# Column mean of the weights from block sums on GpSimd, and the low words' top bits on ScalarE, in an attention and feed-forward kernel

## The chip, the cores and the metric

The kernel runs on one core of a Trainium2 chip. The metric is the device time of one execution in microseconds (us); the kernel before has a median of 963.42 us over 3 runs. The engines are named as in the profile: PE is TensorE (PEld its weight loads), DVE is VectorE, ACT is ScalarE, POOL is GpSimd, SP is the engine that issues most of the DMAs.

## The reference

```python
def reference(**kw):
    # q, k, v: (8 batches, 8 heads, 576 positions, 64), float32
    scores = q @ k^T / 8, masked: heads 0-3 the last 32 positions, heads 4-7 every 32nd position
    x = softmax(scores) @ v           # laid out as (8, 576, 512)
    return _moe_ref(x, g_ln, w_ch1, w_ch2)

def _moe_ref(x, g_ln, w_ch1, w_ch2):  # w_ch1 (512, 2048), w_ch2 (2048, 512): float64 as drawn
    mu = np.mean(x, axis=-1, keepdims=True)
    var = np.mean((x - mu) ** 2, axis=-1, keepdims=True)
    xn = (x - mu) / np.sqrt(var + 1e-06) * g_ln
    ch = np.maximum(xn @ w_ch1, 0.0) @ w_ch2
    return (x + ch).astype(np.float32)
```

The two weights reach the kernel as 64-bit floats, that is as pairs of 32-bit words: a low word and a high word.

## The kernel before, in words

The 8 x 576 rows of x are worked in 9 chunks of 512 rows (c = 0 to 8). The hidden dimension 2048 is worked in 16 blocks of 128 (f = 0 to 15). For each chunk and block, `ffn1` multiplies x by a block of the first weights into one PSUM tile `ph`, ScalarE takes the positive part into `hh` (line 651), VectorE the rest into `hl` (line 652), and one step later `ffn2` multiplies these by the block of the second weights. Weights and x are held as sums of two parts that TensorE multiplies fast, so that each product is three products.

The attention of the later batches is cut into pieces (a generator `pieces`). In every step f one piece stands between `ffn1(f)` and `ffn2(f-1)`: scores, a transposition of the probabilities, the product with v, or a transposition of the result. A piece has work on TensorE and, behind it, on VectorE, ScalarE and GpSimd. Some pieces also turn the next pair's q and k on VectorE (lines 362 to 367).

The weights are taken apart once, in chunk 0, by the class `Split`. A block has two halves: half 0 is its part of the first weights, half 1 of the second. For a half,

- `scaled` (ScalarE, line 188) scales the high word by a power of two into a PSUM tile `p`, of which there is a single buffer;
- `low` (VectorE, line 194) shifts the low word right by 29, in place;
- `magnitude` (VectorE, line 198) puts the two together, and `sign` (VectorE, line 204) adds the sign and writes the 32-bit weight `r`.

For half 0, `by_g` (GpSimd, line 212) multiplies the rows by the layer norm's factors into `wg`. `column_mean` (TensorE, line 219) multiplies `r` by `gmean`, a matrix that holds the factors over 512, so that each column's mean stands in all 128 rows of the PSUM tile `cm`; that takes four products, one for each block of 128 rows, and each of them is two passes in the trace. `centred` (VectorE, line 223) subtracts it from `wg`. `two_parts` writes a half's high part by ScalarE (line 234) and the rest by GpSimd (line 235).

In chunk 0, step f splits block g = f + 2 (`new`) and finishes block f + 1 (`old`), which `ffn1(f+1)` needs next. Blocks 0 and 1 are split by `whole()` ahead of step 0. Each engine keeps the order in which the code is written: the last lines of the kernel tie every instruction to the one before it on its engine. So the order of the calls in the step is the order on each engine. The PSUM tile `cm` and the pieces' PSUM tiles are in chunk 0 turns of one single buffer (`ps_a`): the mean of block g waits until the piece's tile has been read, and the next piece until `centred` has read `cm`.

Of the kernel before, what the change touches and what calls it, by code (L numbers as in the profile page):

```python
# [8 lines left out]
F32 = mybir.dt.float32  # L9
F32R = mybir.dt.float32r  # L10
U32 = mybir.dt.uint32
AF = mybir.ActivationFunctionType
ALU = mybir.AluOpType
AX = mybir.AxisListType
# [5 lines left out]
def kernel(  # L20
# [10 lines left out]
    nc = tc.nc  # L31

    B, H, S, D = q.shape
    DM, DFF = w1.shape
# [38 lines left out]
    mhalf = const.tile([P, 1], F32, name="mhalf")  # L73
    nc.gpsimd.memset(mhalf, -0.5)
    gcol = const.tile([P, NCC], F32, name="gcol")
    gmean = const.tile([P, NCC, P], F32, name="gmean")


    mask_l = const.tile([P, 64], F32, name="mask_l")
# [100 lines left out]
    class Split:  # L180
        def __init__(self, f):
            self.f = f
            self.bits = [t.rearrange("p (f t) -> p f t", t=2) for t in staged.pop(f)]
            self.p, self.w = [None, None], [None, None]

        def scaled(self, i):
# [3 lines left out]
                scale=2.0 ** -112)  # L190

        def low(self, i):
            t = self.bits[i][:, :, 0]
            nc.vector.tensor_scalar(t, t, 29, None, op0=ALU.logical_shift_right)

        def magnitude(self, i):
            t = self.p[i].bitcast(U32)
# [10 lines left out]
        def by_g(self):  # L208
            w = self.w[0].rearrange("p (c f) -> p c f", c=NCC)
            self.wg = tkp.tile([P, DM], F32, tag="tk", name=f"wg{self.f}")  # L210
            self.wgv = self.wg.rearrange("p (c f) -> p c f", c=NCC)
            nc.gpsimd.tensor_tensor(
                out=self.wgv, in0=w, in1=gcol.unsqueeze(2).broadcast_to([P, NCC, P]), op=ALU.mult)

        def column_mean(self):
            w = self.w[0].rearrange("p (c f) -> p c f", c=NCC)
            self.mean = bank(f"cm{self.f}")[:, 0:P]
            for c in range(NCC):
                nc.tensor.matmul(  # L219
                    self.mean, gmean[:, c, :], w[:, c, :], start=(c == 0), stop=(c == NCC - 1))  # L220

        def centred(self):
            nc.vector.tensor_tensor(
                out=self.wgv, in0=self.wgv,
                in1=self.mean.unsqueeze(1).broadcast_to([P, NCC, P]), op=ALU.subtract)

        def two_parts(self, i):
            w = (self.wg, self.w[1])[i]
            t = w_tile(i + 1, self.f, [P, 2, DM], F32R, "w")
            (w1s, w2s)[i][self.f] = t  # L230
            if i == 1 and self.f == NFC - 1:

                w_pools[1].tile([P, 88], F32, name="pad")
            nc.scalar.activation(out=t[:, 0], in_=w, func=AF.Copy)  # L234
            nc.gpsimd.tensor_tensor(out=t[:, 1], in0=w, in1=t[:, 0].bitcast(F32), op=ALU.subtract)  # L235

        def whole(self):
            self.low(0)
# [457 lines left out]
    for i in range(NHP + 3):  # L696
        if i < NHP:
            first[i].s_scores()
        if 2 <= i <= NHP + 1:
            first[i - 2].v_piece()  # L700
            if i < NHP:
                pairs[NHP + i - 2].load_v()
        if i + 1 < NHP:
            first[i + 1].t_rows()
        if 3 <= i:
            first[i - 3].x_piece()
        if 1 <= i <= NHP:
            first[i - 1].p_piece()
            first[i - 1].v_shifted()
        if i < NHP:  # L710
            first[i].s_exp()
        if i == NHP - 1:
            nc.vector.tensor_scalar(
                gmean, gcol.unsqueeze(2).broadcast_to([P, NCC, P]), 1.0 / DM, None, op0=ALU.mult)
        if i == NHP:
            Split(0).whole()
    w_late()
# [66 lines left out]
    for c in range(NCHUNK):  # L784
# [7 lines left out]
        for f in range(NFC):  # L792
            if c == 0:
# [5 lines left out]
                if new:  # L799
                    new.scaled(0)  # L800
                    new.low(0)
                if old:
                    old.centred()
                    old.two_parts(0)
                    old.two_parts(1)
                if new:
                    new.magnitude(0)
                    new.sign(0)
                    new.by_g()
                    new.low(1)  # L810
                    new.scaled(1)
            h = ffn1(c, f)
# [70 lines left out]
```

## Time and profile before

| | |
|---|---|
| median of 3 runs | 963.42 us (960.73 to 964.25) |
| the profiled execution | 962.39 us |
| its span, first to last instruction | 960.6 us |
| mean granted TensorE clock | 0.99 |
| busy: PE, DVE, ACT, POOL | 96%, 44%, 22%, 13% of the span |

The shares are means over the span. Chunk 0's steps run from about 55 to 175 us; behind them the weights are ready, and only the products and the rest of the attention are left. Rows of a timeline give start, length, engine, line, operation, output and inputs; a bracket at the end gives the engine's idle time before the instruction and what ended it. Two instructions that follow each other on an engine overlap a little, so that the step from start to start is shorter than the length.

### The profile page before, as it was taken

Reading aid. Unit: us, or ns where it says so; the run is one execution under the profiler, and the core shown is the slowest. Engines: PE = TensorE matmul, PEld = TensorE weight load, DVE = VectorE, ACT = ScalarE, POOL = GpSimd, SP = SyncE. Lnnn points to the kernel's source line nnn. Section 1 sums busy time; section 2 is a strip of 40 time slices with the busy share of each in tenths; the row PEclk is TensorE's granted clock in tenths of the full one; section 3 lists DMA queues with packets and bytes.
Section 4 is the critical chain, followed back from the end, with each engine's and each line's share of the span. In section 5 each row is a group of like instructions: output and inputs, shape, how many; then the busy total and the mean of one; then the engine's idle time right before and its main releaser. Section 6 shows DMA issues by size and latency. Waiting matters only on the chain.

```text
span 960.6 us, 18743 instructions
## 1 busy us (share of the span) xinstructions
PE 926.0 (96%) x7936; PEld 766.6 (80%) x7936; DVE 427.0 (44%) x857; ACT 212.6 (22%) x337; POOL 127.3 (13%) x150
## 2 busy tenths in 40 slices
PE   6669999999999999999999999999999999999997
PEld 6558787788888888888888888888888888888886
DVE  2689988633454334434543454335432331132112
ACT  3534444121111121211121211121111111110100
POOL 4245556100000001000100010001000000000000
PEclk9879999999999999999999999999999999999999
DMA  9866873442333334333433344334221121002001
GB/s 200 238 158 155 208 212 78 85 101 46 86 63 94 62 85 73 95 61 85 73 95 62 83 74 96 62 64 94 71 38 48 36 76 45 0 1 88 1 1 44
DMA packets 239427, 80.16 MB, mean 83 GB/s; under 512 B 190064, under 2 KB 232688, under 8 KB 239344
## 3 DMA queue, kind: packets, MB, share of 16 engines
q1 hardware_dynamic: 236128, 77.27, 35.3%
q10 hardware_dynamic: 3216, 1.71, 0.8%
q8 instruction: 62, 1.02, 0.5%
q14 instruction: 21, 0.17, 0.1%
HBM read 59.48 MB, written 19.46 MB: 82 GB/s over the span
## 4 chain that ended last, share of the span: by engine, by line
PE 89%; DMA 3%; DVE 3%; SPq 3%; issue 1%; ACT 1%; ACTq 0%; DVEq 0%
PE po L662 40%; PE ph L643 26%; PE ph L647 13%; PE m L464 2%; PE m L396 2%; SPq L299 2%; PE cm L219 2%; PE n L449 1%; PE n L536 1%; DMA rows<-in_k_dram 1%; DMA s<-in_moe_w_ch_dram 1%; DVE p L198 1%; SPq L170 1%; PE av L464 0%; DMA raw<-in_k_dram 0%
## 5 line engine op out<-in xcount | busy, mean ns | idle before, releaser
L662 PE MATMUL po<-w,hh 128*128 128x512 f32 x1152 | 362.2, 396 | 0.0
L652 DVE SCALAR_TENSOR_TENSOR hl<-ph,hh 128x512 fp32r<-128x512 f32 x144 | 99.6, 692 | 465.7 <-ACT hh L651 465.3
L662 PEld LDWEIGHTS po<-w,hh 128*128 128x128 f32 x1152 | 211.2, 188 | 43.6
L643 PE MATMUL ph<-xh,w 128*128 128x512 f32 x576 | 227.2, 395 | 0.2 <-ACT xh L559 0.2
L643 PE MATMUL ph<-xl,w 128*128 128x512 f32 x576 | 225.7, 392 | 0.2 <-DVE xl L561 0.2
L662 PE MATMUL po<-w,hl 128*128 128x512 f32 x576 | 224.9, 391 | 0.0
L651 ACT ACTIVATE hh<-ph 128x512 fp32r<-128x512 f32 x144 | 85.9, 597 | 488.8 <-PE ph L647 488.8
L647 PE MATMUL ph<-xh,w 128*128 128x512 f32 x576 | 154.4, 390 | 0.0
L643 PEld LDWEIGHTS ph<-xl,w 128*128 128x128 f32 x576 | 109.0, 189 | 22.8 <-DVE xl L561 0.5
L643 PEld LDWEIGHTS ph<-xh,w 128*128 128x128 f32 x576 | 108.9, 189 | 22.8 <-ACT xh L559 0.7
L647 PEld LDWEIGHTS ph<-xh,w 128*128 128x128 f32 x576 | 108.5, 188 | 22.7
L662 PEld LDWEIGHTS po<-w,hl 128*128 128x128 f32 x576 | 108.1, 188 | 23.3
L437 POOL TENSOR_TENSOR sm<-sm,mx 128x648 f32<-128x648 f32 (+1 forms) x32 | 40.6, 1269 | 420.2 <-DVE mx L432 409.9
L624 POOL TENSOR_TENSOR rs<-rs,mhalf 128x1 f32<-128x1 f32 x36 | 20.0, 554 | 342.3 <-DVE rs L623 342.3
L440 ACT ACTIVATE sm<-sm 128x648 f32<-128x648 f32 (+1 forms) x32 | 23.8, 744 | 138.7 <-POOL sm L437 138.6
L219 PE MATMUL cm<-r,gmean 128*128 128x128 f32 x128 | 19.3, 299 | 16.2 <-DVE r L204 11.3
L219 PEld LDWEIGHTS cm<-r,gmean 128*128 128x128 f32 x128 | 17.7, 208 | 19.1 <-issue 15.6
L561 DVE TENSOR_TENSOR xl<-n,xh 128x480 fp32r<-128x480 f32 (+2 forms) x36 | 22.7, 666 | 15.4 <-ACT xh L559 15.4
L188 ACT ACTIVATE p<-s 128x512 f32<-128x512 f32 x32 | 20.5, 642 | 34.5 <-DVE r L204 33.1
L432 DVE TENSOR_REDUCE mx<-sm 128x12 f32<-128x648 f32 (+1 forms) x32 | 26.4, 824 | 2.3
L513 DVE TENSOR_TENSOR xo<-m,den 64x64 f32<-64x64 f32 (+3 forms) x120 | 27.1, 290 | 0.1
L235 POOL TENSOR_TENSOR w<-wg,w 128x512 fp32r<-128x512 f32 x16 | 20.7, 1292 | 41.9 <-ACT w L234 38.8
(95 smaller groups left out, 645.9 us busy)
## 6 DMA issues: line engine op xcount, KB each, us to landing
s<-in_moe_w_ch_dram SPq DMA_DIRECT2D x32, 512.0 KB
out_dram<-x SPq DMA_DIRECT2D x32, 256.0 KB
raw<-in_q_dram SPq DMA_DIRECT2D x112, 72.0 KB
raw<-in_k_dram SPq DMA_DIRECT2D x112, 72.0 KB
xds<-xo SPq DMA_DIRECT2D x32, 162.0 KB
v_l<-in_v_dram SPq DMA_DIRECT2D x32, 144.0 KB
xdl<-xo SPq DMA_DIRECT2D x16, 256.0 KB
x<-xdl SPq DMA_DIRECT2D x32, 128.0 KB
```

Source lines behind the costliest of these rows:

```text
L219: nc.tensor.matmul(self.mean, gmean[:, c, :], w[:, c, :], start=(c == 0), stop=(c == NCC - 1))
L235: nc.gpsimd.tensor_tensor(out=t[:, 1], in0=w, in1=t[:, 0].bitcast(F32), op=ALU.subtract)
L432: nc.vector.reduce_max(mx[:, :, 0:nt], sm, axis=AX.X)
L437: nc.gpsimd.tensor_tensor(out=sm, in0=sm, in1=mx[:, :, 0:nt].unsqueeze(3).broadcast_to([P, 2, nt, w]), op=ALU.subtract)
L440: nc.scalar.activation(out=sm, in_=sm, func=AF.Exp, scale=SCALE)
L513: nc.vector.tensor_tensor(out=xo[r, t0:t1, h0:h1].rearrange("p t h d -> p h t d"), in0=av, in1=den[r, h0:h1, t0:t1].unsqueeze(3).broadcast_to(
L561: nc.vector.tensor_tensor(out=dst(xl), in0=src, in1=dst(xh).bitcast(F32), op=ALU.subtract)
L643: nc.tensor.matmul(ph, w1h[:, cc], x[:, cc, :], start=(n == 0), stop=False)
L647: nc.tensor.matmul(ph, w1l[:, cc], xh[:, cc, :], start=False, stop=(cc == NCC - 1))
L651: nc.scalar.activation(out=hh, in_=ph, func=AF.Relu)
L652: nc.vector.scalar_tensor_tensor(out=hl, in0=ph, scalar=0.0, in1=hh.bitcast(F32), op0=ALU.max, op1=ALU.subtract)
L662: nc.tensor.matmul(po[i], hx[:, cs], w, start=(f == 0 and n == 0), stop=(f == NFC - 1 and n == 2))
```

## The change

Three things are changed, all in `Split`.

- The column mean comes from block sums. Behind `by_g` GpSimd adds the four blocks of 128 columns of `wg` in two steps into `bsum` (128x256, then 128x128), and TensorE multiplies the sum once by a constant matrix of 1/512. The matrix `gmean` and the VectorE instruction that filled it are gone.
- `low` runs on ScalarE: it reads the top byte of the low word (one byte in eight), scales and shifts it, and writes the rounded integer to where VectorE wrote the shifted word.
- In a step, half 1 of the old block is finished first, and GpSimd's rest of half 0 comes behind the new block's `by_g` and sums. ScalarE's `low(1)` stands ahead of `scaled(1)`.

```diff
-    gmean = const.tile([P, NCC, P], F32, name="gmean")
+    mean = const.tile([P, P], F32, name="mean")
+    nc.gpsimd.memset(mean, 1.0 / DM)
+    bsum = const.tile([P, 2, P], F32, name="bsum")
+    const.tile([P, P], F32, name="gap")
...
+            self.top = [t.bitcast(U8).rearrange("p (f t) -> p f t", t=8)[:, :, 3] for t in st]
...
         def low(self, i):
-            t = self.bits[i][:, :, 0]
-            nc.vector.tensor_scalar(t, t, 29, None, op0=ALU.logical_shift_right)
+            nc.scalar.activation(
+                out=self.bits[i][:, :, 0], in_=self.top[i], func=AF.Copy, scale=1.0 / 32,
+                bias=-31.0 / 64)
...
                 out=self.wgv, in0=w, in1=gcol.unsqueeze(2).broadcast_to([P, NCC, P]), op=ALU.mult)
+            nc.gpsimd.tensor_tensor(
+                out=bsum, in0=self.wgv[:, 0:2], in1=self.wgv[:, 2:4], op=ALU.add)
+            nc.gpsimd.tensor_tensor(out=bsum[:, 0], in0=bsum[:, 0], in1=bsum[:, 1], op=ALU.add)

         def column_mean(self):
-            w = self.w[0].rearrange("p (c f) -> p c f", c=NCC)
             self.mean = bank(f"cm{self.f}")[:, 0:P]
-            for c in range(NCC):
-                nc.tensor.matmul(
-                    self.mean, gmean[:, c, :], w[:, c, :], start=(c == 0), stop=(c == NCC - 1))
+            nc.tensor.matmul(self.mean, mean, bsum[:, 0], start=True, stop=True)
...
-        if i == NHP - 1:
-            nc.vector.tensor_scalar(
-                gmean, gcol.unsqueeze(2).broadcast_to([P, NCC, P]), 1.0 / DM, None, op0=ALU.mult)
...
                 if old:
+                    old.two_parts(1)
                     old.centred()
-                    old.two_parts(0)
-                    old.two_parts(1)
+                    old.high(0)
                 if new:
                     new.magnitude(0)
                     new.sign(0)
                     new.by_g()
+                if old:
+                    old.rest(0)
+                if new:
                     new.low(1)
                     new.scaled(1)
```

`high(i)` and `rest(i)` are the ScalarE and the GpSimd half of `two_parts(i)`. The instructions of the chunks behind chunk 0, and those of the SP queue, stand as before.

On ScalarE this is step f = 4 before, which splits block 6 and finishes block 5 (`p_6` is the scaled word, `w_5` an old half's high part, from `wg` for half 0 and from `r` for half 1, `hh_4` the output of `ffn1(4)`, `pt_0` the piece's copy):

```order
L188 ACTIVATE p_6_1221<-s_6_924 128x512
L234 ACTIVATE w_5_1225<-wg_1128 128x512
L234 ACTIVATE w_5_1228<-r_5_1198 128x512
L188 ACTIVATE p_6_1237<-s_6_925 128x512
L651 ACTIVATE hh_4_1252<-ph_4_1239 128x512
L454 COPY pt_0_1263<-pp_0_1257 128x640
```

And the same step of the changed kernel (line 199 is `low`, 194 `scaled`, 241 the high part, 666 `hh`):

```order
L194 ACTIVATE p_6_1217<-s_6_923 128x512
L199 ACTIVATE s_6_923<-s_6_923 128x512
L241 ACTIVATE w_5_1220<-r_5_1197 128x512
L241 ACTIVATE w_5_1224<-wg_1124 128x512
L199 ACTIVATE s_6_924<-s_6_924 128x512
L194 ACTIVATE p_6_1235<-s_6_924 128x512
L666 ACTIVATE hh_4_1250<-ph_4_1237 128x512
L469 COPY pt_0_1261<-pp_0_1255 128x640
```

Ahead of `hh_4` there are now six ScalarE instructions in place of four, and the high part of half 1 has moved ahead of that of half 0.

On GpSimd, around the same step, before (`w_5` is the rest of the old block's halves, `wg_1234` the new block's `by_g`):

```order
L212 TENSOR_TENSOR wg_1128<-r_5_1126,gcol 128x512
L235 TENSOR_TENSOR w_5_1225<-wg_1128,w_5_1225 128x512
L235 TENSOR_TENSOR w_5_1228<-r_5_1198,w_5_1228 128x512
L212 TENSOR_TENSOR wg_1234<-r_6_1232,gcol 128x512
L235 TENSOR_TENSOR w_6_1292<-wg_1234,w_6_1292 128x512
```

and of the changed kernel:

```order
L246 TENSOR_TENSOR w_5_1220<-r_5_1197,w_5_1220 128x512
L219 TENSOR_TENSOR wg_1229<-r_6_1227,gcol 128x512
L221 TENSOR_TENSOR bsum<-wg_1229 128x256
L223 TENSOR_TENSOR bsum<-bsum 128x128
L246 TENSOR_TENSOR w_5_1224<-wg_1124,w_5_1224 128x512
L246 TENSOR_TENSOR w_6_1286<-r_6_1263,w_6_1286 128x512
```

The rest of half 0 (`w_5_1224`) has moved behind the new block's factor and the two sums.

## Rows read from the trace of the kernel before

**Rows 1.** From the page: the span, and busy time (share of the span) and instructions of each engine.

```profile
span 960.6 us, 18743 instructions
PE 926.0 (96%) x7936; PEld 766.6 (80%) x7936; DVE 427.0 (44%) x857; ACT 212.6 (22%) x337; POOL 127.3 (13%) x150
```

**Rows 2.** Busy time by stretches of the span; the columns are the stretch, its length, busy us (instructions) of PE, PEld, DVE, ACT and POOL, the granted TensorE clock, the DMA share, GB/s. The stretches are the start of the splitting, steps 1 to 7, steps 8 to 13, and all behind.

```profile
40.00:64.40 24.40, 13.34 (x175) 11.20 (x175) 18.17 (x30) 7.98 (x14) 8.57 (x8) 0.72 0.83 219
64.40:119.00 54.60, 52.44 (x491) 42.49 (x491) 51.01 (x78) 25.16 (x42) 29.85 (x24) 0.97 0.63 154
119.00:163.60 44.60, 44.08 (x348) 36.70 (x349) 40.17 (x67) 21.66 (x36) 24.99 (x21) 1.00 0.61 164
163.60:960.60 797.00, 790.50 (x6271) 652.99 (x6270) 303.11 (x644) 137.67 (x221) 51.63 (x60) 1.00 0.29 63
```

**Rows 3.** Timeline of VectorE in step f = 4, from the sign of block 5's half 1 to the sign of block 6's half 1.

```profile
89.78 0.68 DVE L204 SCALAR_TENSOR_TENSOR r<-s,p 128x512 uint32<-128x512 uint32 x1
90.38 0.40 DVE L194 TENSOR_SCALAR s<-s 128x512 uint32<-128x512 uint32 x1
90.70 0.67 DVE L223 TENSOR_TENSOR wg<-wg,cm 128x512 f32<-128x512 f32 x1
91.30 0.69 DVE L198 SCALAR_TENSOR_TENSOR p<-p,s 128x512 uint32<-128x512 uint32 x1
92.03 0.69 DVE L204 SCALAR_TENSOR_TENSOR r<-s,p 128x512 uint32<-128x512 uint32 x1
92.63 1.13 DVE L194 TENSOR_SCALAR s<-s 128x512 uint32<-128x512 uint32 x1
93.93 0.69 DVE L652 SCALAR_TENSOR_TENSOR hl<-ph,hh 128x512 fp32r<-128x512 f32 x1 [0.17 <-ACT hh L651]
94.54 0.69 DVE L198 SCALAR_TENSOR_TENSOR p<-p,s 128x512 uint32<-128x512 uint32 x1
95.26 0.69 DVE L204 SCALAR_TENSOR_TENSOR r<-s,p 128x512 uint32<-128x512 uint32 x1
```

**Rows 4.** Timeline of ScalarE in the same step.

```profile
90.49 0.64 ACT L188 ACTIVATE p<-s 128x512 f32<-128x512 f32 x1 [5.45 <-DVE r L204]
91.47 0.63 ACT L234 ACTIVATE w<-wg 128x512 fp32r<-128x512 f32 x1 [0.34 <-DVE wg L223]
92.01 0.62 ACT L234 ACTIVATE w<-r 128x512 fp32r<-128x512 f32 x1
92.75 0.63 ACT L188 ACTIVATE p<-s 128x512 f32<-128x512 f32 x1
93.31 0.58 ACT L651 ACTIVATE hh<-ph 128x512 fp32r<-128x512 f32 x1
```

**Rows 5.** Timeline of VectorE: `hl` of steps 0, 7 and 13.

```profile
61.37 0.69 DVE L652 SCALAR_TENSOR_TENSOR hl<-ph,hh 128x512 fp32r<-128x512 f32 x1 [0.81 <-ACT hh L651]
...
116.41 0.69 DVE L652 SCALAR_TENSOR_TENSOR hl<-ph,hh 128x512 fp32r<-128x512 f32 x1 [0.17 <-ACT hh L651]
...
160.25 0.69 DVE L652 SCALAR_TENSOR_TENSOR hl<-ph,hh 128x512 fp32r<-128x512 f32 x1 [0.17 <-ACT hh L651]
```

**Rows 6.** Timeline of TensorE: the first column mean, that of step 4 with the first product of `ffn1(5)` behind it and the piece behind `ffn1(5)`, and the mean of step 13.

```profile
42.21 2.05 PE L219 MATMUL cm<-r,gmean 128*128 128x128 f32 x8 [5.27 <-DVE r L204]
...
94.87 1.05 PE L219 MATMUL cm<-r,gmean 128*128 128x128 f32 x8
95.68 0.48 PE L643 MATMUL ph<-xh,w 128*128 128x512 f32 x1
...
98.52 0.82 PE L536 MATMUL px<-ident,xo 128*128 128x128 f32 x6
...
162.78 1.13 PE L219 MATMUL cm<-r,gmean 128*128 128x128 f32 x8
```

**Rows 7.** A wait between 40 and 165 us: engine, line and what was waited for; us in total, times, the longest.

```profile
DVE wg L223 <- PE cm L219: 3.0, 6, 1.4
```

**Rows 8.** Groups of instructions between 40 and 175 us (that of line 330 between 0 and 40 us), different shapes apart: line, engine, operation, names, shapes, count, busy us and mean ns of one, then the engine's idle time before them.

```profile
L194 DVE TENSOR_SCALAR s<-s 128x512 uint32<-128x512 uint32 x31 | 23.2, 748 | 0.0
L235 POOL TENSOR_TENSOR w<-wg,w 128x512 fp32r<-128x512 f32 x16 | 20.7, 1292 | 41.9 <-ACT w L234 38.8 <-DMA s<-in_moe_w_ch_dram 3.1
L212 POOL TENSOR_TENSOR wg<-r,gcol 128x512 f32<-128x512 f32 x16 | 16.9, 1058 | 13.4 <-DVE r L204 13.4
...
L330 ACT COPY kt_s<-t 128x576 f32<-128x576 f32 x2 | 2.5, 1238 | 0.7 <-PE t L321 0.7
```

**Rows 9.** Timeline of the start: `by_g` of block 0 on GpSimd, and VectorE's `magnitude` of half 0 of blocks 1 and 2.

```profile
42.15 1.16 POOL L212 TENSOR_TENSOR wg<-r,gcol 128x512 f32<-128x512 f32 x1 [7.73 <-DVE r L204]
...
52.52 0.70 DVE L198 SCALAR_TENSOR_TENSOR p<-p,s 128x512 uint32<-128x512 uint32 x1
...
58.72 0.70 DVE L198 SCALAR_TENSOR_TENSOR p<-p,s 128x512 uint32<-128x512 uint32 x1 [1.45 <-ACT p L188]
```

**Rows 10.** Timeline of VectorE in steps 7 to 11: the first and the last of the pieces' operations in them, the first of the statistics of step 11 (lines 619 to 623), and the instruction behind these.

```profile
117.61 0.16 DVE L475 TENSOR_SCALAR den<-av 128x10 f32<-128x10 f32 x1
...
147.59 0.96 DVE L513 TENSOR_TENSOR xo<-av,den 128x768 f32<-128x768 f32 x1
...
149.06 0.69 DVE L619 BATCH_NORM_STATS2 st<-x 128x6 f32<-128x512 f32 x1
...
150.07 0.42 DVE L194 TENSOR_SCALAR s<-s 128x512 uint32<-128x512 uint32 x1
```

More of the change, by code (lines that the diff above doesn't have):

```diff
@@ L11 @@
 U32 = mybir.dt.uint32
+U8 = mybir.dt.uint8
 AF = mybir.ActivationFunctionType
@@ L182, in __init__ @@
             self.f = f
-            self.bits = [t.rearrange("p (f t) -> p f t", t=2) for t in staged.pop(f)]
+            st = staged.pop(f)
+            self.bits = [t.rearrange("p (f t) -> p f t", t=2) for t in st]
+            self.top = [t.bitcast(U8).rearrange("p (f t) -> p f t", t=8)[:, :, 3] for t in st]
             self.p, self.w = [None, None], [None, None]
@@ L225, in centred, with high @@
                 in1=self.mean.unsqueeze(1).broadcast_to([P, NCC, P]), op=ALU.subtract)
-        def two_parts(self, i):
+        def high(self, i):
             w = (self.wg, self.w[1])[i]
@@ L234, in two_parts, with rest @@
             nc.scalar.activation(out=t[:, 0], in_=w, func=AF.Copy)
+        def rest(self, i):
+            w = (self.wg, self.w[1])[i]
+            t = (w1s, w2s)[i][self.f]
             nc.gpsimd.tensor_tensor(out=t[:, 1], in0=w, in1=t[:, 0].bitcast(F32), op=ALU.subtract)
+        def two_parts(self, i):
+            self.high(i)
+            self.rest(i)
         def whole(self):
```

## The prediction

> **What bounds the kernel now.** I read the shares first, then the stretches, then one step row by row. By the shares TensorE is the bound, 926.0 of 960.6 us [rows 1]. The stretches say where that is so. Behind 163.6 us TensorE is busy for 790.5 of 797.0 us and the change touches nothing there, so that part is a constant and only the moment counts at which it begins. In steps 1 to 7 of chunk 0 VectorE is as full as TensorE: 51.01 against 52.44 of 54.6 us. In steps 8 to 13 TensorE is, 44.08 of 44.6, with VectorE at 40.17. [...]
>
> One step shows what runs beside TensorE. Half 1's `sign` on VectorE starts at 89.78 and frees the only buffer of `p`; ScalarE's `scaled` follows at 90.49, VectorE's `magnitude` at 91.30 (held by `low` and `centred` ahead of it), `sign` at 92.03, ScalarE's `scaled(1)` at 92.75, `hh` behind it on the same engine at 93.31, `hl` at 93.93, `magnitude(1)` at 94.54, the next `sign` at 95.26 [rows 3, 4]. The reader is to see that this closes on itself: 5.48 us for a step without VectorE work of a piece, whatever TensorE does. The second `low`, 1.13 us long, lies wholly in the wait for `hh` [rows 3]. From the `hl` of step 0 to that of step 7 it is 55.04 us [rows 5], 7 x 5.48 = 38.4 plus 16.7 for the pieces' VectorE work and waits: in this stretch the loop sets the pace, not TensorE. From step 7 to 13 it is 43.84 us; there `centred` waits for the column mean, which is most of the 3.0 us in 6 waits [rows 7], and TensorE sets the pace.
>
> **The change part by part.** *Column mean.* Eight passes take 0.81 us (94.87 to 95.68) [rows 6]; two take 0.20. TensorE saves 0.61 us in each of 14 steps, 8.5 us in all. That is worth something where TensorE sets the pace, and nothing in steps 1 to 7.
>
> *Sums on GpSimd.* The trace has no such shape. Two dense inputs of 512 cost 1.29 us (line 235), 1.06 with one of them a repeated column (line 212) [rows 8]. Taken in proportion to the columns, with some 0.13 fixed, 256 and 128 columns cost 0.71 and 0.42, together 1.13. Below, they can't be free; above, each could cost as much as 512, 2.6 in all. I take 1.13, since both instructions have a fraction of the columns. In a step, the changed GpSimd does the rest of half 1, `by_g` (1.04 beside 1.06) and the sums ahead of the mean. Counted from the `sign` that opens the step, half 1's high part ends at 2.4, the rest at 3.7, `by_g` at 4.8, the sums at 5.9. TensorE, ahead of the loop in steps 1 to 7, may wait for them there (in step 4 it asked for the mean 1.56 us behind `hh`, at 94.87). But with the mean (0.2) and `ffn1` behind it, 2.84 us long (95.68 to 98.52) [rows 6], TensorE is through at 9.0, and the loop worked out below has its next `hh` at 5.92 + 3.97 = 9.9. So they are hidden by 0.9 us; without that cover all of it would stand on the path.
>
> *Sums at the start.* There nothing hides them. In block 0 the mean began with `by_g` at 42.2 [rows 6, 9]. Now ScalarE's `low` stands ahead of `scaled` (0.55), and `by_g` (1.16) and the sums (1.13) ahead of the mean, which needs 0.5 in place of 2.05 at the low clock: 0.55 + 2.29 - 1.55 = 1.3 us later for all behind it, up to block 1's transpositions. Block 1's `magnitude`, at 52.52 [rows 9], loses VectorE's `low` ahead of it (0.5) and is 0.8 later; the same replacement, 2.29 - 1.55, makes its mean and `centred` 1.5 later; then ScalarE's `low` adds 0.55 ahead of the `magnitude` of block 2 at 58.72. The `hl` of step 0 comes 2.05 us later, at 63.4.
>
> *`low` on ScalarE, and the order.* The byte read and the integer write are not in the trace. Nearest is an instruction of the same 512 elements from SBUF to SBUF, 0.62 long and 0.54 from start to start [rows 4]; `scaled` itself reads every second word and takes 0.64. Dearest is the copy whose writes stand 72 bytes apart, 1.24 us for 576 elements [rows 8]; at that rate a `low` costs 1.1. I take 0.62, since the new step of 8 bytes is the one `scaled` reads with. [...]
>
> Now the loop again, in us from the opening `sign`: `scaled` 0.71, `low` 1.25, ending 1.87; `magnitude` 1.90 (0.38 later than before: the two ScalarE steps follow each other, where VectorE's `low` and `centred` had run beside `scaled`); `sign` 2.62 to 3.31. ScalarE meanwhile does half 1's high part at 1.79, half 0's at 2.33, `low(1)` at 2.87, and so `scaled(1)` at 3.41, `hh` at 3.97, `hl` 4.59, `magnitude(1)` 5.20, `sign` 5.92. The loop is 0.44 us longer, though VectorE has two instructions fewer in it: both its `low`s lay beside a wait for ScalarE. In steps 1 and 3, where the softmax's exponential holds ScalarE beforehand, ScalarE's six instructions up to `hh` take 6 x 0.54 = 3.26 from `scaled`, where it was 2.68: 0.58 more. In step 2, where `centred` waited for the mean, I take 0.2.
>
> **The sum.** Steps 1 to 7: 2 x 0.58 + 0.2 + 4 x 0.44 = 3.1 us more. `hl` of step 7: 63.4 + 55.0 + 3.1 = 121.6 (116.4 before). Steps 8 to 13: 6 x 5.92 = 35.5; the pieces' VectorE work in them, from the first to the last of 12 instructions [rows 10], 6.24 less four bubbles of 0.12 that it fills, 5.8; and the statistics of steps 11 and 12, 1.0 each (149.06 to 150.07) of which 0.25 outlasts `low`: 41.8 us, against 43.84 before. TensorE alone would need 44.08 - 6 x 0.61 = 40.4, so the loop now sets the pace here too, and only 2.0 of the 3.7 us that TensorE saves are had. `hl` of step 13: 163.4 (160.25). The mean of step 13 came 2.53 us behind it (162.78), held by the piece's reading of the shared PSUM buffer, and stays so: 165.9, plus 0.2 in place of 0.81: `ffn1(14)` begins at 166.1 in place of 163.6. Behind that TensorE sets the pace as before. So **2.5 us more**: 964.9 by the profiled execution's own 962.39, which lies 1.0 under the median; by the median 965.9.
>
> **Rivals.** *All of TensorE's time comes back.* For it: TensorE is at 96% [rows 1], and the second stretch. It needs a loop that never outlasts TensorE; against it the 55.04 us of steps 1 to 7 [rows 5], 7.9 a step, where TensorE after the change needs about 6.7. Price: 8.5 less about 1.8 at the start, 956.7. Even with a `low` that costs ScalarE nothing, the loop of steps 1 to 7 would stay, and the time be about 963.4 + 1.5 - 3.7 = 961.2.
>
> *ScalarE's `low` is slow* (strided write, or the byte). At 1.1 us there is 0.48 more twice a step, both in line ahead of `hh`: 14 x 0.96 = 13.4, 979.3; halfway, 972.6. Over 0.78 us it decides, by 14 x 2 x 0.16 = 4.5.
>
> *The sums come late.* With two sums at 2.6 us they are ready at 7.4 and TensorE is through with `ffn1` at 10.4, 0.5 behind the loop: that much in each step without VectorE work of a piece (4, 8, 12), and 2 x 1.47 = 2.9 at the start. Some 4.4 more, 970.3; it decides from 2.0 us for the two.
>
> **How the numbers follow.** The forecast with its own range 963.5 to 968.5: 0.54. All of TensorE's time: 0.08. A gain or loss in between, with `low` cheaper than 0.62 or the start covered, 960 to 963.5: 0.14. Slow `low`, 969 to 980: 0.13. Late sums: 0.11. A measurement of this kernel can tell about 0.5%, 4.8 us. Faster takes the second case and a little of the third, 0.09; slower the slow `low`, most of the late sums and the upper end of the forecast, 0.29; the rest is no change. The range 959.5 to 974 leaves out all of TensorE's time and the upper half of the slow `low`.
>
> **What would show it.** Right: column means of two passes; VectorE's busy time between 64 and 119 us down to about 41, with TensorE waiting more; in a piece-free step 5.9 us from `sign` to `sign`, ScalarE without a gap from `scaled` to `hh`; `hl` of step 0 near 63.4, of step 7 near 121.6; the stretch behind `ffn1(14)` unchanged. Wrong: `hl` of step 7 at or before 116.4; a `low` far from 0.62 us; sums over 1.3 us a block together, with TensorE waiting for GpSimd ahead of the mean.

## The result, and the profile after

The changed kernel takes 967.8 us (median of 20 runs, 962.89 to 972.56), the kernel before, run beside it, 961.62 (20 runs). The ratio is 1.0056, with a 95% interval of 1.0045 to 1.0068: 5.4 us slower, about the 0.5% that this measurement can tell (the two medians by themselves stand 6.2 us apart, which the interval covers; the text goes by the ratios, since the runs of before differ from one set to the next). The forecast was 2.5 us slower, a ratio of 1.0026. Its 965.9 lies close to 967.8 in part by luck, because the kernel before came out 1.8 us lower here than in the runs from which the forecast was made. The profiled execution of the changed kernel took 970.14 us, 2.3 over the median.

The page of the changed kernel: span, busy time of the engines, and the granted clock in 40 slices (compare [rows 1]).

```profile
span 968.0 us, 18554 instructions
PE 921.0 (95%) x7840; PEld 758.5 (78%) x7840; DVE 406.2 (42%) x824; ACT 228.5 (24%) x369; POOL 143.5 (15%) x183
PEclk9769999999999999999999999999999999999999
```

TensorE has 96 passes fewer, VectorE is 20.8 us less busy, ScalarE 15.9 and GpSimd 16.2 more: the work has gone where the change moved it, and the span is 7.4 us longer. The stretches that answer to [rows 2], cut at the same events (columns as there):

```profile
40.00:70.86 30.86, 14.63 (x164) 11.15 (x165) 17.42 (x26) 13.82 (x24) 12.99 (x14) 0.63 0.70 182
70.86:126.20 55.34, 46.75 (x447) 35.84 (x446) 39.91 (x62) 30.36 (x55) 35.45 (x37) 0.99 0.61 151
126.20:170.86 44.66, 42.75 (x308) 34.50 (x309) 31.55 (x54) 27.61 (x48) 31.02 (x34) 0.92 0.63 164
170.86:968.00 797.14, 790.34 (x6270) 652.93 (x6268) 303.45 (x645) 137.97 (x221) 51.66 (x61) 1.00 0.29 63
```

The last is 797.14 us long, 797.0 before: all the time is lost ahead of it. In the second VectorE is busy for 39.91 us where it was 51.01, and TensorE for 46.75 where it was 52.44: neither engine is full any more, and the stretch is no shorter. In the third the granted clock is 0.92; it was 1.00. The `hl` of steps 0, 7 and 13, VectorE (compare [rows 5]):

```profile
65.55 0.69 DVE L667 SCALAR_TENSOR_TENSOR hl<-ph,hh 128x512 fp32r<-128x512 f32 x1 [1.24 <-ACT hh L666]
...
123.59 0.69 DVE L667 SCALAR_TENSOR_TENSOR hl<-ph,hh 128x512 fp32r<-128x512 f32 x1 [1.22 <-ACT hh L666]
...
168.00 0.69 DVE L667 SCALAR_TENSOR_TENSOR hl<-ph,hh 128x512 fp32r<-128x512 f32 x1 [1.21 <-ACT hh L666]
```

Steps 1 to 7 take 58.04 us (55.04 before), steps 8 to 13 44.41 (43.84). The first of the three stands 4.18 us later than before; 1.3 of that lies ahead of the third normalization of attention, in a stretch whose length differs from profile to profile (see the experiments). Step 4, VectorE and then ScalarE (compare [rows 3, 4]):

```profile
95.16 0.68 DVE L211 SCALAR_TENSOR_TENSOR r<-s,p 128x512 uint32<-128x512 uint32 x1
...
97.13 0.70 DVE L205 SCALAR_TENSOR_TENSOR p<-p,s 128x512 uint32<-128x512 uint32 x1 [0.71 <-ACT s L199]
...
99.77 0.69 DVE L667 SCALAR_TENSOR_TENSOR hl<-ph,hh 128x512 fp32r<-128x512 f32 x1 [1.21 <-ACT hh L666]
...
101.10 0.69 DVE L211 SCALAR_TENSOR_TENSOR r<-s,p 128x512 uint32<-128x512 uint32 x1
```

```profile
95.86 0.63 ACT L194 ACTIVATE p<-s 128x512 f32<-128x512 f32 x1 [5.45 <-DVE r L211]
96.43 0.67 ACT L199 ACTIVATE s<-s 128x512 uint32<-128x512 uint8 x1
97.00 0.61 ACT L241 ACTIVATE w<-r 128x512 fp32r<-128x512 f32 x1
97.52 0.61 ACT L241 ACTIVATE w<-wg 128x512 fp32r<-128x512 f32 x1
98.04 0.67 ACT L199 ACTIVATE s<-s 128x512 uint32<-128x512 uint8 x1
98.62 0.60 ACT L194 ACTIVATE p<-s 128x512 f32<-128x512 f32 x1
99.16 0.57 ACT L666 ACTIVATE hh<-ph 128x512 fp32r<-128x512 f32 x1
```

From `sign` to `sign` it is 5.94 us in place of 5.48. ScalarE runs without a gap from `scaled` to `hh`, VectorE waits 0.71 us for a low word and 1.21 for `hh`: what was a wait of VectorE filled with its own low words is now ScalarE's line, one instruction behind the other. The groups of the new instructions (columns as in [rows 8]):

```profile
L199 ACT ACTIVATE s<-s 128x512 uint32<-128x512 uint8 x32 | 21.2, 666 | 0.0
...
L221 POOL TENSOR_TENSOR bsum<-wg 128x256 f32<-128x256 f32 x16 | 11.7, 732 | 1.3
L223 POOL TENSOR_TENSOR bsum<-bsum 128x128 f32<-128x128 f32 x16 | 7.3, 458 | 1.3
```

The start, GpSimd and TensorE, block 0: the product by g, the two sums, and the mean that waits for them (compare [rows 6, 9]).

```profile
44.01 1.04 POOL L219 TENSOR_TENSOR wg<-r,gcol 128x512 f32<-128x512 f32 x1 [8.82 <-DVE r L211]
45.13 0.73 POOL L221 TENSOR_TENSOR bsum<-wg 128x256 f32<-128x256 f32 x1
45.93 0.46 POOL L223 TENSOR_TENSOR bsum<-bsum 128x128 f32<-128x128 f32 x1
...
46.44 0.80 PE L227 MATMUL cm<-bsum,mean 128*128 128x128 f32 x2 [8.18 <-POOL bsum L223]
```

And one place that the prediction had not looked at: TensorE at the end of step 7, the column mean and the first products of `ffn1(8)` behind it, and the clock around it (a stretch, its length, PE busy, granted clock, DMA share, GB/s).

```profile
126.20 0.62 PE L227 MATMUL cm<-bsum,mean 128*128 128x128 f32 x2 [1.97 <-DVE xo L528]
...
127.05 0.63 PE L658 MATMUL ph<-xl,w 128*128 128x512 f32 x1
127.48 0.63 PE L658 MATMUL ph<-xh,w 128*128 128x512 f32 x1
```

```profile
120.00:125.00 5.00, 3.96 (x92) 1.00 0.65 105
125.00:130.00 5.00, 3.79 (x11) 0.66 0.91 264
...
155.00:160.00 5.00, 3.76 (x12) 0.71 0.53 129
```

The 0.66 and the 0.71 are means: from 127 to 129 us the granted clock is 0.50, from 130 to 131 it is 1.00. Behind a wait of 1.97 us the products of 512 columns stand 0.43 us apart, with the clock at 0.50; with it at 1.00 they stand 0.23 apart (123.62 and 123.85). The same follows the wait of 1.90 us at 156.24 (0.50 from 158 to 160 us). `hl` of step 8 comes 8.11 us behind that of step 7 (7.17 before).

### The profile page after: what moved, and what is told of

The parts are those of the page before. It is cut to its first block, busy times and chain, and to the rows that moved or that the text cites. A ratio compares the mean times of both kernels' runs of the same rounds, so it can differ in the third digit from the quotient of the medians.

```text
span 968.0 us, 18554 instructions
## 1 busy us (share of the span) xinstructions
PE 921.0 (95%) x7840; PEld 758.5 (78%) x7840; DVE 406.2 (42%) x824; ACT 228.5 (24%) x369; POOL 143.5 (15%) x183
## 4 chain that ended last, share of the span: by engine, by line
PE 83%; DVE 0%; ACT 0%; issue 0%; DVEq 0%
PE po L677 38%; PE ph L658 25%; PE ph L662 12%; PE m L479 2%; PE m L411 2%; PE n L464 1%; PE n L551 1%; DVE x L683 0%; PE px L646 0%; ACT p L194 0%; PE pp L464 0%; PE px L551 0%; ACT s L199 0%; ACT w L241 0%; PE cm L227 0%
## 5 line engine op out<-in xcount | busy, mean ns | idle before, releaser
L658 PEld LDWEIGHTS ph<-xh,w 128*128 128x128 f32 x576 | 110.0, 191 | 23.1 <-ACT xh L574 0.7
L662 PEld LDWEIGHTS ph<-xh,w 128*128 128x128 f32 x576 | 109.7, 190 | 23.3
L227 PE MATMUL cm<-bsum,mean 128*128 128x128 f32 x32 | 7.9, 334 | 27.5 <-POOL bsum L223 17.4
L227 PEld LDWEIGHTS cm<-bsum,mean 128*128 128x128 f32 x32 | 5.5, 205 | 32.0 <-POOL bsum L223 23.2
L205 DVE SCALAR_TENSOR_TENSOR p<-p,s 128x512 uint32<-128x512 uint32 x32 | 22.3, 697 | 16.0 <-ACT s L199 11.3
```

The lines of the kernel that those rows point to most:

```text
L205: nc.vector.scalar_tensor_tensor(out=t, in0=t, scalar=3, in1=self.bits[i][:, :, 0], op0=ALU.logical_shift_left, op1=ALU.bitwise_or)
L658: nc.tensor.matmul(ph, w1h[:, cc], x[:, cc, :], start=(n == 0), stop=False)
L662: nc.tensor.matmul(ph, w1l[:, cc], xh[:, cc, :], start=False, stop=(cc == NCC - 1))
```

## The experiments

Theory A: the low words in ScalarE's line lengthen the loop of VectorE and ScalarE; that costs steps 1 to 7 what they lost, and takes most of what TensorE saves in steps 8 to 13. Theory B: the price is in the exposed sums at the start and in the fall of TensorE's clock. The table has each kernel's stages in us, from the starts of instructions in its profile: "start" is from the third normalization of attention (`den`, 35.85 before, 37.18 after) to the `hl` of step 0, the others from `hl` to `hl`. What lies ahead of that `den` varies from 34.38 to 38.23 between the profiles without order and is left out; behind the `hl` of step 14 all have 793.1 to 794.0 us. "Sum" is the difference of the four to before; it comes from one profile of each kernel. "Ratio" is that of the timed runs, with its interval. Each set of runs has its own runs of the kernel before beside it, so times of different sets are compared by their ratios.

| kernel | start | steps 1–7 | 8–13 | 14 | sum | ratio |
|---|---|---|---|---|---|---|
| before | 25.52 | 55.04 | 43.84 | 7.09 | | |
| changed | 28.37 | 58.04 | 44.41 | 6.44 | +5.8 | 1.0056 (1.0045–1.0068) |
| e1 low words on VectorE | 27.92 | 55.44 | 41.92 | 6.30 | +0.1 | 1.0001 (0.9989–1.0014) |
| e2 before + ScalarE low words | 25.63 | 58.06 | 45.12 | 7.08 | +4.4 | 1.0040 (1.0019–1.0062) |
| e3 changed, old mean | 26.16 | 58.01 | 45.91 | 7.12 | +5.7 | 1.0041 (1.0027–1.0056) |
| e4 low words a step ahead | 28.87 | 54.14 | 41.13 | 6.39 | −1.0 | 1.0004 (0.9987–1.0022) |
| e5 clock held | 28.36 | 58.06 | 42.03 | 6.41 | +3.4 | 1.0031 (1.0017–1.0045) |
| e6 old mean at the start | 26.13 | 58.06 | 42.05 | 6.40 | +1.2 | 1.0016 (1.0004–1.0029) |
| e7 = e4 and e6 | 27.49 | 54.18 | 41.11 | 6.41 | −2.3 | 0.9959 (0.9946–0.9973) |
| e8 before + sums, old order | 27.92 | 59.92 | 45.16 | 7.20 | +8.7 | 1.0091 (1.0072–1.0111) |
| e9 changed, again | 28.35 | 58.06 | 42.92 | 6.41 | +4.2 | 1.0059 (1.0039–1.0079) |
| e10 = e5, again | 28.35 | 58.03 | 42.06 | 6.42 | +3.4 | 1.0026 (1.0011–1.0041) |
| e11 = e3 and e4 | 27.66 | 54.69 | 43.72 | 7.10 | +1.7 | 1.0011 (0.9997–1.0026) |

**e1, one part undone: the low words.**

```diff
-            nc.scalar.activation(
-                out=self.bits[i][:, :, 0], in_=self.top[i], func=AF.Copy, scale=1.0 / 32,
-                bias=-31.0 / 64)
+            t = self.bits[i][:, :, 0]
+            nc.vector.tensor_scalar(t, t, 29, None, op0=ALU.logical_shift_right)
```

> The changed kernel with the low words back on VectorE; the sums, the one product and the new order of the split's parts stay. Theory A (the low words on ScalarE lengthen the loop of VectorE and ScalarE, and what TensorE saves in steps 8 to 13 is then of no use): the loop from sign to sign, 5.94 us in step 4 of the changed kernel, goes back to between 5.5 and 6.2 (a low word on VectorE takes 0.62 us alone and over 1 us where it lies beside GpSimd, and GpSimd's rest now ends later), the granted clock of steps 8 to 13 stays below 1.00 as long as TensorE waits there; some 2 to 4 us less than the changed kernel, so a ratio of 1.001 to 1.004 to the kernel before. Theory B (the price lies in the sums at the start and in the fall of TensorE's clock, not in ScalarE's line): steps 1 to 7 get shorter by under 1 us and the ratio stays at 1.005.

Theory A, and more than the 2 to 4 us that it expected: all 5.4 us are gone (962.7 us, ratio 1.0001). The clock, expected below 1.00 in steps 8 to 13, is at 1.00 there; in this profile no wait of TensorE between 95 and 165 us is as long as 1.4 us, and none has a fall behind it. VectorE in step 4 of this kernel (a low word alone takes 0.40 us here, not the 0.62 expected):

```profile
93.52 0.68 DVE L210 SCALAR_TENSOR_TENSOR r<-s,p 128x512 uint32<-128x512 uint32 x1
94.12 0.40 DVE L200 TENSOR_SCALAR s<-s 128x512 uint32<-128x512 uint32 x1
...
96.38 0.70 DVE L200 TENSOR_SCALAR s<-s 128x512 uint32<-128x512 uint32 x1
97.69 0.69 DVE L666 SCALAR_TENSOR_TENSOR hl<-ph,hh 128x512 fp32r<-128x512 f32 x1 [0.62 <-ACT hh L665]
...
99.02 0.69 DVE L210 SCALAR_TENSOR_TENSOR r<-s,p 128x512 uint32<-128x512 uint32 x1
99.63 1.23 DVE L200 TENSOR_SCALAR s<-s 128x512 uint32<-128x512 uint32 x1
```

The loop is 5.50 us again (93.52 to 99.02), and the second low word stands in the wait for `hh`. TensorE's saving now arrives: steps 8 to 13 and 14 are 2.7 us shorter than before. The start takes 2.4 of it back, and steps 1 to 7 another 0.4.

**e2, that part alone.** The kernel before with line 199 and the byte view, nothing else.

```diff
+            st = staged.pop(f)
...
+            self.top = [t.bitcast(U8).rearrange("p (f t) -> p f t", t=8)[:, :, 3] for t in st]
...
-            t = self.bits[i][:, :, 0]
-            nc.vector.tensor_scalar(t, t, 29, None, op0=ALU.logical_shift_right)
+            nc.scalar.activation(
+                out=self.bits[i][:, :, 0], in_=self.top[i], func=AF.Copy, scale=1.0 / 32,
+                bias=-31.0 / 64)
```

> The kernel before with one part of the change alone: the low words on ScalarE. The mean stays four products, without sums, in the old order. Theory A: the loop of step 4 is 5.48 us before and gets 0.3 to 0.5 longer, steps 1 to 7 take 2 to 3.5 us more than their 55.0, steps 8 to 13 stay bound by TensorE at 43.8, the start takes about 1 us more (two low words in ScalarE's line); together 3 to 4.5 us, a ratio of 1.003 to 1.005. Theory B: at most 1 us, a ratio of 1.000 to 1.001.

Theory A again: 966.18 us, 3.9 slower by the ratio, and steps 1 to 7 take 58.06, as in the changed kernel. A miss in it: the start loses 0.1, not 1, and steps 8 to 13 are not at TensorE's 43.8 but at 45.12. Step by step they come near the longer of the two kernels: 8.94 us in step 11, as in the changed kernel (8.95), and 7.72 in step 12, as before. That would make 44.3; the other 0.8 stands in steps 8 and 9 (7.43 each, 7.17 and 7.06 before) and 13 (6.82, 6.60 before), and its cause stays open. The clock did not fall there.

**e3, the mean undone.** Four products with `gmean`, no sums; low words and order as changed.

```diff
-            nc.gpsimd.tensor_tensor(out=bsum, ...)
-            nc.gpsimd.tensor_tensor(out=bsum[:, 0], ...)
...
-            nc.tensor.matmul(self.mean, mean, bsum[:, 0], start=True, stop=True)
+            for c in range(NCC):
+                nc.tensor.matmul(
+                    self.mean, gmean[:, c, :], w[:, c, :], start=(c == 0), stop=(c == NCC - 1))
...
```

> The changed kernel with the mean of before (four products from the weights as they are, no sums on GpSimd); the low words stay on ScalarE and the order is the new one. Theory A: steps 1 to 7 as in the changed kernel, 57.5 to 58.5 us; steps 8 to 13 bound by TensorE again at about 44, with the granted clock at 1.00 there; the start 1 to 2 us shorter than in the changed kernel, since nothing waits for sums: 1 to 2 us less in all, a ratio of 1.003 to 1.005. Theory B (the sums at the start and the clock are the price): steps 8 to 13 shorter than the changed kernel's 44.4 by more than 1.5 us, and a ratio of 1.000 to 1.002.

The time is Theory A's (966.49 us), and beside e2 the order is worth nothing without the sums that these intervals could tell: 1.0041 and 1.0040. Steps 8 to 13 were expected at 44 with the clock at 1.00, and were 45.91. The mean of step 7 and the first products of `ffn1(8)`, first in e3, then in e2:

```profile
122.96 1.60 PE L223 MATMUL cm<-r,gmean 128*128 128x128 f32 x8 [1.93 <-DVE xo L525]
...
124.78 0.63 PE L655 MATMUL ph<-xl,w 128*128 128x512 f32 x1
125.21 0.63 PE L655 MATMUL ph<-xh,w 128*128 128x512 f32 x1
```

```profile
122.78 1.13 PE L223 MATMUL cm<-r,gmean 128*128 128x128 f32 x8 [1.94 <-DVE xo L517]
...
123.98 0.39 PE L647 MATMUL ph<-xl,w 128*128 128x512 f32 x1
124.21 0.39 PE L647 MATMUL ph<-xh,w 128*128 128x512 f32 x1
```

Two waits of the same length, and the clock fell behind one of them (0.43 us from product to product, a granted clock of 0.81 as the mean of 125 to 130 us) and not behind the other (0.23, and 1.00). Step 8 took 8.77 us there and 7.43 here. So a fall needs no sums. These are two programs; e9 below has the same program with and without a fall in this place.

**e4, the low words one step ahead on ScalarE**, where ScalarE waits anyway (in the steps not listed below the call stands behind the piece).

```diff
+    def look_ahead(g):
+        nonlocal ahead
+        ahead = Split(g) if g < NFC else None
+        if ahead:
+            ahead.low(0)
+            ahead.low(1)
+
+    look_ahead(WAHEAD)
...
-                    new.low(0)
...
-                    new.low(1)
...
+            if c == 0 and f in (0, 2, 3, 6, 7, 10, 11):
+                look_ahead(g + 1)
```

> The changed kernel with both low words of a block made one step earlier on ScalarE, in its idle time or behind the rest of the step, so that the loop of VectorE and ScalarE no longer contains them. TensorE's saving and the sums stay. Theory A: the loop goes back to 5.4 to 5.6 us in steps without a piece of attention, steps 1 to 7 to 55 to 56 us (58.0 in the changed kernel), steps 8 to 13 to 41 to 43.5; 4 to 7 us less than the changed kernel, a ratio of 0.998 to 1.002. Theory B: the clock falls in steps 8 and 12 as in the changed kernel, or more, since TensorE waits as much; under 2 us less than the changed kernel, a ratio of 1.004 or more.

Theory A: 963.0 us, 5.0 under the changed kernel by the ratios. The same instructions on the same engine cost the steps nothing once they are out of the line: both low words stand behind `hh`.

```profile
94.78 0.63 ACT L194 ACTIVATE p<-s 128x512 f32<-128x512 f32 x1 [0.41 <-DVE r L211]
95.35 0.58 ACT L666 ACTIVATE hh<-ph 128x512 fp32r<-128x512 f32 x1
...
96.40 1.22 ACT L199 ACTIVATE s<-s 128x512 uint32<-128x512 uint8 x2
```

Steps 1 to 7 are 0.9 us shorter than before (54.14, where 55 to 56 were expected), steps 8 to 13 2.7. The start is 0.5 longer than in the changed kernel, with the two low words of block 2 now ahead of the loop.

**e5 and e10, the clock held.** The changed kernel with products that add nothing, where TensorE is about to wait.

```diff
+    zero = const.tile([P, P], F32, name="gap")
+    nc.vector.memset(zero, 0.0)
...
+        if c == 0 and f in (2, 6, 10):
+            for n in range(7):
+                nc.tensor.matmul(
+                    po[NT - 1], zero.bitcast(F32R), w2h, start=False, stop=False)
```

> The changed kernel with seven further products of 512 columns, with weights of zero (they add nothing), behind the second product of steps 2, 6 and 10, where TensorE then waits 1.9 to 2.5 us for VectorE before the column mean. The wait shrinks by what they take (about 1.6 us at full clock). Theory C (a wait of about 2 us lets TensorE's clock fall to half, and that costs 1.5 us in step 8 and some in step 12 of the changed kernel's profile): no stretch below 1.00 between 120 and 165 us, steps 8 to 13 take 42 to 43 us (44.4 in the changed kernel), ratio 1.003 to 1.004. Theory D (the fall hangs on the execution and what it costs is small in most; the loop of VectorE and ScalarE is the price of steps 8 to 13 too): the median stays within 0.1% of the changed kernel's, ratio 1.005 to 1.006.

Theory C, for its size: 965.19 us; steps 8 to 13 take 42.03 with the clock at 1.00 from 120 to 165 us, and `ffn1(8)` runs at 0.23 us a product. The added products ahead of the mean of step 7, and the stretch behind it (columns as in the result, where the same stretch has 0.66):

```profile
122.16 1.80 PE L683 MATMUL po<-w,gap 128*128 128x512 f32 x7
124.21 0.46 PE L228 MATMUL cm<-bsum,mean 128*128 128x128 f32 x2 [0.26 <-DVE xo L529]
```

```profile
125.00:130.00 5.00, 5.00 (x26) 1.00 1.14 306
```

More work on TensorE made the kernel 2.4 us faster, by the ratios. This was repeated beside the changed kernel on one chip:

> The changed kernel with the seven products of weights zero ahead of the three longest waits, once more, beside the changed kernel on the same chip. Theory C: no fall between 120 and 165 us, steps 8 to 13 at 42.0; 0.5 to 2.5 us less than the changed kernel beside it, about the share of executions with a fall times 2.4 us; ratio 1.0025 to 1.005. Theory D (the difference of the first runs was the chip's): the same ratio as the changed kernel within 0.05%.

965.6 us against 968.6: 3.0 less, with 42.06 us for steps 8 to 13. That is more than the 0.5 to 2.5 expected, and a little more than the 2.4 us which the two falls of the first profile cost; the intervals (1.0011 to 1.0041, 1.0039 to 1.0079) leave room for that. The granted clock of the timed runs points the same way for executions that have no profile: its mean is 0.982 and 0.981 in the two sets of the changed kernel (20 and 9 runs), and 0.984 in both sets with the waits filled (9 and 12).

**e9, the changed kernel again.**

> The changed kernel once more, unchanged, for the price of the clock's falls. Its first profiled execution needed 44.4 us for steps 8 to 13, with the granted clock at half behind two waits of 1.90 and 1.97 us; a variant with the same steps needed 42.05 us without a fall behind waits of 1.89 and 1.98 us. Theory C (the falls come in part of the executions): the profiled execution has steps 8 to 13 at 42.0 us if no stretch of 120 to 165 us is below 1.00, and 1.3 to 2.5 us more if one or two are; ratio 1.0045 to 1.006. If steps 8 to 13 take over 43.5 us without a fall of the clock, the clock isn't what it was.

Theory C in kind: one fall, behind the wait of 1.99 us that ends at 151.92, and 42.92 us for steps 8 to 13, 0.87 above the undisturbed 42.05, where 1.3 to 2.5 were expected. Behind the wait of 1.94 us, in the place where the first profile of this same kernel has a fall, there is none:

```profile
123.41 0.46 PE L227 MATMUL cm<-bsum,mean 128*128 128x128 f32 x2 [1.94 <-DVE xo L528]
...
123.94 0.39 PE L658 MATMUL ph<-xl,w 128*128 128x512 f32 x1
124.17 0.39 PE L658 MATMUL ph<-xh,w 128*128 128x512 f32 x1
```

So the fall belongs to the execution. Another came earlier, behind 2.50 us at 90.41 (the products of `ffn1(4)` stand 0.43 us apart), and cost nothing: step 4 took 9.34 us, 9.32 in the first profile, because the loop, not TensorE, sets the pace there.

**e6, the old mean for the two blocks ahead of the loop.**

```diff
-            nc.gpsimd.tensor_tensor(out=bsum, ...)
-            nc.gpsimd.tensor_tensor(out=bsum[:, 0], ...)
+            if self.f > 1:
+                nc.gpsimd.tensor_tensor(out=bsum, ...)
+                nc.gpsimd.tensor_tensor(out=bsum[:, 0], ...)
...
+            if self.f > 1:
+                nc.tensor.matmul(self.mean, mean, bsum[:, 0], start=True, stop=True)
+                return
+            for c in range(NCC):
+                nc.tensor.matmul(
+                    self.mean, gmean[:, c, :], w[:, c, :], start=(c == 0), stop=(c == NCC - 1))
...
```

> The changed kernel with the mean of before (four products of the weights as they are) for the two blocks that are made before the loop; from block 2 on sums and one product. Theory: the sums of these two blocks are exposed, and from the third normalization of attention in the start to the remainder of step 0 it takes 25.6 to 26.3 us instead of 28.4 (25.5 before); the rest is as in the changed kernel: 2 to 2.8 us less, a ratio of 1.0025 to 1.0035. Rival: the wait is only handed on to the products of step 0 or to GpSimd's later parts; under 1 us less, ratio 1.005.

The start is 26.13 us, 2.24 shorter: that is what the sums cost there. 964.05 us, 1.0016: a little more gained than expected. No fall of the clock came in steps 8 to 13 of this profile, behind waits of 1.89 and 1.98 us, which may be the rest.

**e7, the low words one step ahead and the old mean at the start**, the edits of e4 and e6 together.

> Low words one step ahead on ScalarE, and the mean of before for the two blocks ahead of the loop; sums and one product from block 2 on. Theory A with the price of the start: start 26 to 27 us from the third normalization to the remainder of step 0 (28.9 with the low words ahead alone), steps 1 to 7 54 to 55, steps 8 to 13 41 to 42, step 14 6.4: 3 to 4.5 us less than before, a ratio of 0.9955 to 0.997. Rival: a shorter start meets later weights or transfers in the first steps, and the gain is under 1 us: ratio 0.999 to 1.000.

959.32 us, 0.9959: faster than both kernels. The steps are as expected; the start, 27.49, is 0.5 over its range: the two low words of block 2 stand ahead of the loop, as in e4.

**e11, the low words one step ahead and the old mean everywhere**, the edits of e3 and e4 together.

> Low words one step ahead on ScalarE with the mean of before (four products, no sums) in all blocks: what TensorE's saving is worth once the loop is short. Theory A: steps 1 to 7 54 to 55 us, steps 8 to 13 bound by TensorE again at 43.5 to 44, step 14 at 7.1, start 25.6 to 27 from the third normalization; 0.5 us more to 1.5 us less than before, ratio 0.9985 to 1.0005, and so 3 to 4 us slower than the kernel with sums from block 2 on (0.9959). Rival: the sums are worth nothing there either, the low words one step ahead make all of that gain: ratio 0.996.

963.23 us. With the loop short, TensorE sets the pace in steps 8 to 13 again (43.72), and the sums with the one product are worth 4.0 us by the stages (e7 has −2.3 for +1.7), 5.0 by the ratios. The ratio, 1.0011, is just above the range expected, as the start (27.66) is.

**e8, the sums in the old order**, low words on VectorE: the kernel before with the mean of the changed one. Against e1 only the order differs.

```diff
-                    old.two_parts(1)
                     old.centred()
-                    old.high(0)
+                    old.two_parts(0)
+                    old.two_parts(1)
...
-                if old:
-                    old.rest(0)
-                if new:
```

> The kernel before with the sums on GpSimd and the one product, low words on VectorE and the parts of the split in the old order (both remainders of GpSimd ahead of the product by g). If the new order is needed for the sums, GpSimd reaches them about 1.3 us later in steps without a piece of attention, TensorE waits for them there (1.3 to 2.5 us before the column mean), and it is 2 to 4 us slower than with the new order: a ratio of 1.002 to 1.004. If the order is worth nothing: 0.999 to 1.001, as with the new order and the low words on VectorE (1.0001).

972.59 us, 8.7 over e1 by the ratios and 8.6 by the stages, where 2 to 4 were expected: the direction was right, the size was not. Steps 2 and 5 lose 1.8 and 2.7 us against e1, but steps 8 to 10, 13 and 14 lose 0.6 to 1.0 each as well. GpSimd and TensorE in step 4:

```profile
98.02 1.30 POOL L245 TENSOR_TENSOR w<-wg,w 128x512 fp32r<-128x512 f32 x1 [4.10 <-ACT w L240]
99.28 1.48 POOL L245 TENSOR_TENSOR w<-r,w 128x512 fp32r<-128x512 f32 x1
100.72 1.04 POOL L218 TENSOR_TENSOR wg<-r,gcol 128x512 f32<-128x512 f32 x1
...
102.78 0.45 POOL L222 TENSOR_TENSOR bsum<-bsum 128x128 f32<-128x128 f32 x1
...
103.29 0.49 PE L226 MATMUL cm<-bsum,mean 128*128 128x128 f32 x2 [2.48 <-POOL bsum L222]
```

Both rests stand ahead of the product by g, and the mean waits 2.48 us for the second sum. Part of the price may be the clock once more: behind this wait, and behind one of 2.44 us that ends at 77.09, the products of `ffn1` come to stand 0.43 us apart, and these are the falls of steps 5 and 2. In steps 8 to 13 the clock stays at 1.00, behind waits of up to 1.89 us for the sums.

## Why the prediction was right, and where it was not

**The loop, right.** 5.94 us for 5.92 said; steps 1 to 7 58.04 from `hl` to `hl`, for 55.0 + 3.1 = 58.1. It is not two errors that cancel: steps 1 to 7 grew by 0.57, 0.06, 0.56, 0.47, 0.48, 0.39 and 0.47 us, where 0.58, 0.2, 0.58 and four times 0.44 were said. ScalarE without a gap; VectorE 39.91 us busy for about 41. That the low words are the cause is shown by e1 (5.50, the loss gone), e2 (they alone: 58.06) and e4 (the same instructions out of the line: 54.14).

**The durations, right.** A low word took 0.666 us (0.62 said), the sums 1.19 a block (1.13). No row of before had a write of ScalarE at 8 bytes; measured, its 0.666 us stand beside 0.627 of `scaled` and 0.61 of the dense high part in step 4. The 0.13 us fixed in the working of the sums was the author's estimate, and no row showed it; a line through the two sums, 458 ns for 128 columns and 732 for 256, has 2.1 ns a column and 0.18 us fixed.

**Sums hidden in the steps, right, with its condition.** 0.9 us of cover was said, in the new order. In step 4 TensorE does wait 1.40 us for the second sum, and the loop is 5.94 us all the same (the wait ends with the mean at 101.39). With the old order the cover is gone, and the price is 8.6 us, falls of the clock included (e8 against e1).

**The start: a term too small.** Said +2.05, measured +2.85 between the same events. e6 puts 2.24 of it on the sums, where the working had 2 x 0.74 = 1.48: that is nearly the whole miss. From half 0's `sign` of block 0 to `centred` it is 43.24 to 47.27 now and 41.38 to 44.37 before: 1.04 more, where the working had 0.74 (2.29 − 1.55); block 1 shows the same (4.04 and 2.98). The step that failed is in the main "needs 0.5 in place of 2.05": two passes took 0.80 us with the granted clock at 0.50 (46.4 to 47.3 us), not a quarter of the 2.05 that eight took, also at 0.50 (42.0 to 44.2 us before; the 0.72 of [rows 2] is the mean of the stretch). About 0.1 more is in the sums, from whose start to the mean it is 1.31 us (45.13 to 46.44), not 1.13.

**Steps 8 to 13: the term that failed.** The loop was said to set the pace at 41.8 us. Undisturbed it does, 42.05 (e6), 42.03 and 42.06 (e5, e10). What the working left out is that the granted clock fell behind some of TensorE's waits (to 0.50 behind the 1.97 us that end at 126.20): [rows 2] showed 1.00 here, where TensorE hardly waited, and the sum priced the longer waits at nothing. The trace of before had a sign of it: behind a wait of 2.79 us that ends at 63.45 the products of `ffn1(1)` come to stand 0.43 us apart (0.50 granted from 65 to 67 us), and [rows 2] has 0.97 for steps 1 to 7. In the first profile two falls cost 2.4 us (44.41), in the second one cost 0.87, and the kernel with the waits filled is 2.4 us faster by the ratios in e5 and 3.0 by the medians in e10. So the 5.4 us are about 3.4 that the stages show without a fall (28.36, 58.06, 42.03 and 6.41 in e5) and, as the difference, about 2 from the clock; the forecast had 2.5 of the first and none of the second. The 2 us that were missing and the 1.8 by which the kernel before came out lower point opposite ways in the forecast's 965.9: that it lies so near is luck, the +3.1 of steps 1 to 7 is not. What decides whether a wait of 1.9 to 2.5 us ends with a fall, stays open.

**The rivals.** "All of TensorE's time comes back" fell as said: even with the low words back on VectorE, the start takes 2.4 of it (e1). Of its 8.5 us, 3.4 came back in steps 8 to 14 (e4), once the loop was out of the way, and a gain was left only when the start was spared too (e7). The slow low word and the late sums did not occur. The forecast's most likely case, no change within 0.5%, is left by a hair in the ratio, and the interval holds both sides of it; the chance of slower was 0.29.

## What to carry to other kernels

Before an instruction moves to a less busy engine, look at what stands in that engine's line: here two instructions of 0.67 us went from waits of VectorE into ScalarE's part of a closed loop, and the 20.8 us by which VectorE became less busy gained nothing; one step earlier on the same engine they cost the steps nothing. Work saved on the bound engine is worth its time only in stretches where that engine sets the pace, and where it doesn't, the saving becomes waiting. Here the granted clock fell to 0.50 behind waits of 1.90 and 1.97 us in the first profile of the changed kernel and stayed at 1.00 behind one of 2.53, and products that add nothing, put into the waits, made the kernel 2.4 us (e5) and 3.0 us (e10) faster. In the kernel before it fell behind a wait of 2.79 us. Sums that wait for another engine belong where that engine is ahead, and not in the start, where nothing covers them and they cost 2.24 us (e6).

## What had not been expected of the hardware

- Waits of 1.93 and 1.94 us in the same place (e3, e2), one with the products of 512 columns 0.43 us apart behind it and one with 0.23; in the first profile of the changed kernel a wait of 2.53 us had no fall behind it, in its second profile one of 2.50 had. A fall cost 1.5 us in steps 8 and 9 (8.11 and 6.40, where e9 has 7.00 and 5.97), 0.9 in step 12 (8.22, where e6 has 7.36), and nothing where the loop left room.
- Two passes of 128 columns behind a wait took 0.80 us at a granted clock of 0.50 (46.44) and 0.46 at 1.00 (123.41 in e9), when eight took 2.05 and 1.13: a quarter of the passes took 0.4 of the time.
- VectorE's shift of a low word took 0.40, 0.70 and 1.23 us within one step (e1). The two long ones began while a rest of GpSimd was running (95.49 to 96.79 and 99.28 to 100.57), and each ended 0.29 us after that rest; the short one began with GpSimd idle. In the kernel before it is the same (92.63 to 93.76, with a rest from 92.18 to 93.48).
